# Part-filled PV rounds released and zero filler matmuls issued where a planner sees TensorE thinly used

## The chip, the cores and the metric

One core of a Trainium2 chip. The time is device microseconds (us) of one execution, lower is better; a time told here is the median of several executions of the same program. Only executions in the undisturbed ("fast") state occurred. Engines are named as the profile names them: PE is TensorE, ACT ScalarE, DVE VectorE, POOL GpSimd, SP SyncE.

## The reference

A layer normalisation of x (2048 x 512) feeds two branches: multi-query attention with 32 heads of 16 channels that share one key and one value head, and an MLP (512 to 1792 to 512). The result is `x + attention * silu(MLP)`.

```python
xn = layernorm(x)
q = (xn @ wq) in 32 heads of 16; k = xn @ wk; v = xn @ wv      # one k, one v
s = softmax(q k^T / 4) v, heads joined, @ wo
g = silu( silu(xn @ w1) @ w2 )
return x + s * g
```

The bulk is 32 x 2048 x 2048 exponentials of scores. ACT computes about three quarters of the score blocks (1556 of 2048 blocks of 128 x 512) and DVE the other 492, by a chain of integer operations.

## The kernel before

The Python code does not emit instructions directly. A planner inside it simulates the engines with fixed planned durations, decides at each step what each engine does next, and emits the resulting five fixed instruction streams with the semaphore waits that they need. A change of one rule can therefore move instructions on every engine.

PE does three kinds of work in the steady state: scores (`do_S`, up to four row tiles at once), jobs (projections and MLP, in rounds of four column tiles) and PV rounds (`do_pv`: up to four probability blocks times the values, four column tiles at once, all into one bank of PSUM, the memory that PE writes its results to, `ps` in the profile's lines). A PV round with fewer than four blocks is held back for up to 1 us:

```python
def pv_round(t):
    ... # for each of the four column tiles: the first block that is ready, into got
    if len(got) < 4 and nleft[g] > 0 and t - old < HOLD and a_pressure() < NPA - 2:
        return ("wait", min(soon, old + HOLD))
    return ("go", got)
```

At each step PE takes scores if they are due, else a job, else a PV round, else the tail; if there is nothing it waits until the next thing is ready:

```python
def pe_step():
    ...
    if pr and pr[0] == "go" and (a_pressure() >= NPA - 2):
        col = ("pv", pr[1])
    elif jr[0] == "go":
        col = ("job", jr[1])
    elif pr and pr[0] == "go":
        col = ("pv", pr[1])
    elif tr and tr[0] == "go":
        col = ("tail", None)
    ...
    if st["assigned"] < 3 and "zer" in pl.lastw and ...:      # start only: warm-up
        n = st["warm"] = st.get("warm", 0) + 1
        pl.place(PE, T_COLD if n <= N_COLD else MM, lambda pe: pe.matmul(
            bank(7), lhsT=zer_sb[:, 0:P], rhs=zer_sb[:, :], start=True, stop=True), ["zer"], [("ps", 7)], ...)
```

The planner knows a slow ("cold") matmul only there: the first `N_COLD` warm-up matmuls are planned at `T_COLD` (427 ns), everything later at `MM` (216 ns). In the profile before, the warm-up's weight loads stand 0.43 us apart until 6.73 us, and the five from 7.12 us on take 0.96 us together. Two PSUM banks, 5 and 7, form a pool for jobs and for DVE's score blocks.

## Time and profile before

| | before |
|---|---|
| median of 4 runs of the comparison | 778.38 us (776.87 to 780.08) |
| span of the profiled execution | 777.3 us |
| ACT idle in it | 28.7 us |
| of that, from 40 us to the last exponential | 8.0 us |
| mean granted PE clock of it | 0.985 |

How to read it: ACT, the busiest engine, has 748.6 us of work to do, so as long as that work stays the same only its idle time can be won. The granted clock is 1.0 at full PE clock and 0.5 at half: from 40 to 760 us of this profile it reads 0.50 for 3.4 us each from 280.1, 563.4 and 747.8 us on (a "window" in what follows), for 6.8 us, two windows, from 420.1 us on, and 1.00 elsewhere.

### The profile page before, as it was taken

What the parts mean: (1) busy time and instruction counts of PE and PEld (TensorE: products, weight loads), DVE (VectorE), ACT (ScalarE), POOL (GpSimd) and SP (SyncE); (2) the same over time, 40 slices, a digit from 0 to 9 for tenths busy, and PEclk for the clock granted to TensorE, in tenths of its full rate; (3) what the DMA queues carried; (4) which work ended last, traced back from release to release, by engine and by line L of the source; (5) the groups of instructions that cost most, each with busy time, mean ns of one, the idle gap of its engine ahead of it and who ended that gap; (6) DMA issues with size and microseconds to landing.
All of it is one profiled execution on the core that took longest, in us unless ns stands there. A gap on an engine that the chain in (4) does not pass through costs nothing.

```text
span 777.3 us, 19793 instructions
## 1 busy us (share of the span) xinstructions
PE 706.3 (91%) x8600; PEld 202.2 (26%) x8600; DVE 737.9 (95%) x1290; ACT 748.6 (96%) x760; POOL 19.9 (3%) x46
## 2 busy tenths in 40 slices
PE   8899899899989899899988998999998899999985
PEld 3322222222222222222222222222222222222221
DVE  8699999999999989999998999999999999999995
ACT  5899999999999999999998999999999999999995
POOL 5400000000000000000000000000000000000000
PEclk9999999999999999999998999999999999999999
DMA  9300000000000100000000010000000000000000
GB/s 312 84 1 2 2 1 2 2 2 2 1 2 16 29 14 2 2 2 2 2 1 1 16 42 2 2 1 2 3 2 1 15 16 29 2 1 2 2 1 28
DMA packets 11428, 12.55 MB, mean 16 GB/s; under 512 B 1808, under 2 KB 10768, under 8 KB 11344
## 3 DMA queue, kind: packets, MB, share of 16 engines
q1 hardware_dynamic: 10288, 11.28, 4.5%
q8 instruction: 68, 1.11, 0.6%
q10 hardware_dynamic: 1056, 0.03, 0.1%
q14 instruction: 16, 0.13, 0.1%
HBM read 8.95 MB, written 2.10 MB: 14 GB/s over the span
## 4 chain that ended last, share of the span: by engine, by line
ACT 80%; DVE 10%; PE 9%; issue 1%; POOL 0%; ACTq 0%; DVEq 0%
ACT pa_sb L1170 76%; DVE db_sb L869 4%; DVE ds_sb L903 3%; ACT t_sb L521 3%; PE ps L963 3%; PE ps L693 3%; PE ps L394 2%; PE ps L1146 1%; ACT t_sb L544 1%; DVE stats_sb L355 0%; DVE u_sb L523 0%; DVE f_sb L980 0%; PE ps L410 0%; POOL v_sb L478 0%; DVE qt_sb L501 0%
## 5 line engine op out<-in xcount | busy, mean ns | idle before, releaser
L1170 ACT ACTIVATE pa_sb<-ps 128x1024 bf16<-128x1024 f32 (+1 forms) x681 | 732.2, 1358 | 8.2 <-PE ps L693 4.4
L869 DVE TENSOR_SCALAR db_sb<-ps 128x512 uint16<-128x512 f32 x492 | 326.2, 681 | 17.3 <-PE ps L693 15.6
L903 DVE TENSOR_SCALAR ds_sb<-db_sb 128x2048 uint16<-128x2048 uint16 x492 | 321.6, 679 | 1.1
L693 PE MATMUL ps<-qt_sb,kt_sb 32*128 32x512 bf16 x2048 | 269.6, 387 | 53.4 <-ACT pa_sb L1170 42.7
L963 PE MATMUL ps<-ds_sb,v_sb 128*32 128x512 bf16 x1968 | 264.0, 387 | 4.0 <-DVE ds_sb L903 3.3
L963 PE MATMUL ps<-pa_sb,v_sb 128*32 128x512 bf16 x1556 | 255.3, 390 | 3.3 <-DVE ds_sb L903 2.1
L693 PEld LDWEIGHTS ps<-qt_sb,kt_sb 32*128 32x128 bf16 x2048 | 68.5, 91 | 337.8 <-ACT pa_sb L1170 275.4
L963 PE MATMUL ps<-db_sb,v_sb 128*32 128x512 bf16 x492 | 131.7, 393 | 2.9 <-DVE f_sb L980 2.4
L963 PEld LDWEIGHTS ps<-ds_sb,v_sb 128*32 128x32 bf16 x1968 | 66.3, 95 | 67.3 <-issue 35.6
L963 PEld LDWEIGHTS ps<-pa_sb,v_sb 128*32 128x32 bf16 x1556 | 62.4, 95 | 56.1 <-issue 35.4
L394 PE MATMUL ps<-xnT_sb,w_sb 128*32 128x512 bf16 x896 | 76.0, 390 | 0.1
L394 PE MATMUL ps<-w_sb,u_sb 128*32 128x512 bf16 x896 | 74.9, 384 | 0.0
L521 ACT ACTIVATE t_sb<-ps 128x512 bf16<-128x512 f32 x56 | 44.9, 802 | 1.9 <-PE ps L394 1.9
L523 DVE SCALAR_TENSOR_TENSOR u_sb<-t_sb,ps 128x512 bf16<-128x512 bf16 x56 | 38.0, 678 | 0.2 <-ACT t_sb L521 0.2
L963 PEld LDWEIGHTS ps<-db_sb,v_sb 128*32 128x32 bf16 x492 | 32.3, 95 | 20.5 <-issue 9.5
L980 DVE STREAM_TRANSPOSE f_sb<-ps 128x512 f32<-128x512 f32 x32 | 22.6, 707 | 7.7 <-PE ps L963 7.7
L394 PEld LDWEIGHTS ps<-xnT_sb,w_sb 128*32 128x32 bf16 x896 | 19.5, 94 | 29.0 <-issue 20.2
L394 PEld LDWEIGHTS ps<-w_sb,u_sb 128*32 128x32 bf16 x896 | 18.6, 94 | 29.2 <-issue 23.5
L394 PE MATMUL ps<-xnT_sb,wq_sb 128*32 128x512 bf16 x256 | 20.4, 384 | 0.2 <-DVE u_sb L523 0.2
L394 PE MATMUL ps<-wo_sb,on_sb 128*32 128x512 bf16 x256 | 19.1, 382 | 0.0
L984 DVE TENSOR_TENSOR otr_sb<-f_sb,rcp_sb 128x256 bf16<-128x256 f32 x32 | 13.2, 413 | 0.0
L544 ACT ACTIVATE t_sb<-ps 128x512 bf16<-128x512 f32 x16 | 13.0, 810 | 0.0
(42 smaller groups left out, 156.1 us busy)
## 6 DMA issues: line engine op xcount, KB each, us to landing
w_sb<-in_B_w_dram SPq DMA_DIRECT2D x2, 1792.0 KB, 13.5
xr_sb<-in_A_x_dram SPq DMA_DIRECT2D x16, 128.0 KB, 2.3
out_dram<-ob_sb SPq DMA_DIRECT2D x16, 128.0 KB, 1.7
ds_sb<-in_A_x_dram SPq DMA_DIRECT2D x3, 512.0 KB, 6.7
ds_sb<-in_A_x_dram SPq DMA_DIRECT2D x4, 128.0 KB, 2.6
wq_sb<-in_A_wq_dram SPq DMA_DIRECT2D x1, 512.0 KB, 4.8
wo_sb<-in_A_wo_dram SPq DMA_DIRECT2D x1, 512.0 KB, 15.3
kt_sb<-kt_sb SPq DMA_DIRECT2D x4, 64.0 KB, 2.4
```

The costliest lines, as they stand in the source:

```text
L394: last = h.matmul(bank(b)[32 * j:32 * (j + 1), :], lhsT=lhs(j), rhs=rhs, start=start, stop=stop, tile_position=(0, 32 * j), skip_group_che ...
L521: t1 = Task(AC, 477.0, lambda a: a.activation(t_sb[:, k, :], bank(b), ACT.Tanh, scale=0.5), [("ps", b)], [("t", k)], 0)
L523: t2 = Task(DV, T_P, lambda v: v.scalar_tensor_tensor(out=u_sb[:, ft, :], in0=t_sb[:, k, :], scalar=1.0, in1=bank(b), op0=ALU.add, op1=ALU ...
L544: t1 = Task(AC, 477.0, lambda a: a.activation(t_sb[:, k, :], bank(b), ACT.Tanh, scale=0.25), [("ps", b)], [("t", k)], 0)
L693: return pe.matmul(bank(b), lhsT=kt_sb[32 * i:32 * i + 32, g % 2, kt * P:(kt + 1) * P], rhs=qt_sb[32 * i:32 * i + 32, (g // 2) % NQR, :], ...
L869: bt.P[i] = pl.add(Task(DV, T_P, lambda v, b=b, i=i, bb=bt.b: v.tensor_scalar(db_sb[:, bb, i * NQ:(i + 1) * NQ], bank(b), 128.0 * LOG2E, 1 ...
L903: pl.add(Task(DV, T_SH, lambda v, s=s, j=j, bb=bt.b: v.tensor_scalar(ds_sb[:, s, :], db_sb[:, bb, :], SHIFT[j], None, op0=ALU.add), [("Db" ...
L963: h = pe.matmul(bank(OB)[32 * i:32 * (i + 1), :], lhsT=lhs, rhs=rhs, start=s0, stop=s1, tile_position=(0, 32 * i), skip_group_check=True)
L980: t1 = pl.add(Task(DV, T_TR, lambda v: v.transpose(f_sb[:, k, :], bank(OB)), [("ps", OB)], [("F", k)], 1, [norm.get(("m", g - 2))]))
L984: t3 = pl.add(Task(DV, 332.0, lambda v: v.tensor_tensor(o3[:, :, val:val + DH], f3[:, :, val:val + DH], rcp_sb[:, k, :].unsqueeze(2).to_br ...
L1146: pl.place(PE, T_COLD if n <= N_COLD else MM, lambda pe: pe.matmul(bank(7), lhsT=zer_sb[:, 0:P], rhs=zer_sb[:, :], start=True, stop=True), ...
L1170: op = pl.place(AC, 0.8333 * NQ * n + T_AF, lambda a: a.activation(pa_sb[:, s, 0:n * NQ], ps[:, b0 * 512:(b0 + n) * 512], ACT.Exp), [("ps" ...
```

## The change

The intent is to keep the PE clock up; that this rule does it is what the experiments test. Where the planned use of PE over the last 3 us is a half or less, a part-filled PV round goes at once, and if PE has nothing else, a round of four zero matmuls goes into a free bank of the pool. Besides, the planner is told of 14 cold warm-up matmuls instead of 10.

```diff
-T_TP, T_COLD, N_COLD = 56.0, 427.0, 10
+T_TP, T_COLD, N_COLD = 56.0, 427.0, 14
+LOW_USE, USE_WIN = 0.5, 3000.0
-            if len(got) < 4 and nleft[g] > 0 and t - old < HOLD and a_pressure() < NPA - 2:
+            if len(got) < 4 and nleft[g] > 0 and t - old < HOLD and a_pressure() < NPA - 2 and pe_share(t) > LOW_USE:
                 return ("wait", min(soon, old + HOLD))
+        def pe_share(t):          # planned use of PE over the last USE_WIN ns
+            ...
+            return s / USE_WIN
+        def fill_bank(t):         # None above LOW_USE, else a free pool bank
+            ...
+        def do_fill(t, b):
+            pl.place(PE, MM, lambda pe: col4(pe, b, lambda j: zer_sb[:, 32 * j:32 * (j + 1)], zer_sb[:, :], True, True),
+                     ["zer"], [("ps", b)], t0=pe_start(t, "C"))
+            ...
             elif tr and tr[0] == "go":
                 col = ("tail", None)
+            elif st["assigned"] > 0 and not tail["made"]:
+                fb = fill_bank(t)
+                if fb is not None:
+                    col = ("fill", fb)
```

More of the change, by code (lines that the diff above doesn't have):

```diff
@@ L1098, in a_pressure @@
             return sum(1 for b in pa_busy if b)
+        def pe_share(t):
+            s = 0.0
+            for op in reversed(pl.order[PE]):
+                if op.end <= t - USE_WIN:
+                    break
+                s += op.end - max(op.t0, t - USE_WIN)
+            return s / USE_WIN
+        def fill_bank(t):
+            if "zer" not in pl.lastw or pe_share(t) > LOW_USE:
+                return None
+            for b in pool_free:
+                if pl.ready(PE, ["zer"], [("ps", b)]) <= t:
+                    return b
+            return None
+        def do_fill(t, b):
+            pl.place(PE, MM, lambda pe: col4(pe, b, lambda j: zer_sb[:, 32 * j:32 * (j + 1)], zer_sb[:, :], True, True),
+                     ["zer"], [("ps", b)], t0=pe_start(t, "C"))
+            pl.mode = "C"
+            st["fills"] = st.get("fills", 0) + 1
         def pe_step():
@@ L1134, in pe_step @@
                     do_job(t, col[1])
+                elif col[0] == "fill":
+                    do_fill(t, col[1])
                 else:
```

## The prediction

> **What bounds the kernel now.** I began with the first part of the page, the busy shares, and then the chain of waits that ended last.
>
> ```profile
> span 777.3 us, 19793 instructions
> ...
> PE 706.3 (91%) x8600; PEld 202.2 (26%) x8600; DVE 737.9 (95%) x1290; ACT 748.6 (96%) x760; POOL 19.9 (3%) x46
> ...
> ACT 80%; DVE 10%; PE 9%; issue 1%; POOL 0%; ACTq 0%; DVEq 0%
> ```
>
> ScalarE (ACT) is the bound: it is idle for 777.3 - 748.6 = 28.7 us in all, and the chain lies on it for 80% of the span. TensorE (PE) looks 91% full, but the table of waits has it waiting for ACT's exponentials for longer than for all else together:
>
> ```profile
> PE ps L693 <- ACT pa_sb L1170: 42.7, 113, 1.0
> ```
>
> So PE has slack, and its work costs time only where it makes ACT wait. I therefore split ACT's 28.7 us by stretches of 20 us. Up to 20 us ACT is busy for 10.70 of 20 (9.3 us idle: loads, normalisation, transposes, first keys), from 20 to 40 us for 18.05 (1.95 idle), and after its last exponential, at about 767.9 us, it is idle for 9.4 us (last normalisation, output product, write). That leaves 28.7 - 9.3 - 1.95 - 9.4 = 8.0 us for the 728 us in between. This is all that a steadier PE could win in the steady state. The stretches of 20 us (PE, weight loads, DVE, ACT, POOL, then PEclk):
>
> ```profile
> 240.00:260.00 20.00, 18.03 (x239) 5.16 (x235) 20.00 (x36) 18.82 (x22) 0.00 (x0) 1.00 0.05 15
> ...
> 280.00:300.00 20.00, 19.66 (x231) 5.16 (x227) 17.54 (x30) 19.34 (x22) 0.00 (x0) 0.91 0.01 2
> ...
> 380.00:400.00 20.00, 17.45 (x221) 5.14 (x222) 19.95 (x34) 18.25 (x20) 0.00 (x0) 1.00 0.00 1
> ...
> 420.00:440.00 20.00, 19.73 (x215) 5.07 (x219) 17.56 (x32) 17.68 (x19) 0.00 (x0) 0.83 0.05 15
> ...
> 560.00:580.00 20.00, 17.77 (x209) 4.86 (x208) 18.96 (x34) 19.32 (x20) 0.00 (x0) 0.91 0.00 1
> ...
> 740.00:760.00 20.00, 16.50 (x168) 4.12 (x166) 18.88 (x34) 19.07 (x18) 0.00 (x0) 0.91 0.00 1
> ```
>
> Two of these six lose ACT time at the full clock (240 and 380 us: 1.18 and 1.75 us, with DVE at 20.00 and 19.95 of 20, so DVE led there). In the other four PE's granted clock fell. The worst, in steps of 2 us:
>
> ```profile
> 416.00:418.00 2.00, 1.05 (x11) 0.31 (x11) 2.00 (x5) 2.00 (x4) 0.00 (x0) 1.00 0.00 0
> 418.00:420.00 2.00, 1.37 (x18) 0.38 (x16) 0.99 (x2) 2.00 (x3) 0.00 (x0) 1.00 0.00 0
> 420.00:422.00 2.00, 2.00 (x16) 0.38 (x16) 1.97 (x4) 1.71 (x2) 0.00 (x0) 0.52 0.00 0
> 422.00:424.00 2.00, 2.00 (x18) 0.55 (x18) 1.80 (x6) 2.00 (x3) 0.00 (x0) 0.50 0.00 0
> 424.00:426.00 2.00, 2.00 (x24) 0.40 (x16) 0.77 (x2) 0.86 (x1) 0.00 (x0) 0.50 0.00 0
> 426.00:428.00 2.00, 2.00 (x26) 0.63 (x22) 1.78 (x3) 1.13 (x1) 0.00 (x0) 0.77 0.00 0
> ```
>
> Read it downwards: PE is lightly used for 4 us while it waits for ACT (11 and 18 matmuls instead of about 24), then runs at half clock for about 6.8 us, and at the end of that ACT starves. The timeline puts 0.29 + 2.01 = 2.30 us of ACT idle into this stretch, 0.16 + 0.51 = 0.67 into the one at 280 us, 0.17 + 0.51 = 0.68 into that at 564 us, and the stretch at 747 us shows 0.93. Sum: 4.6 us of ACT idle that goes with a halved clock. That is the target of the change.
>
> [...]one window of 3.4 us at half clock in 20 us gives 1 - 0.5 x 3.4/20 = 0.915 (the rows say 0.91), two give 0.83 (as at 420 us).[...] In the trace the weight loads of the warm-up stand at 2.03, 2.46, 2.89, 3.31 us and so on up to 6.73, 0.43 apart, and the five from 7.12 us on take 0.96 us together.[...]
>
> **The change part by part.** The order of instructions of both built kernels gives the counts.
>
> Work: scores (2048 matmuls), PV (492 + 1968 + 1556), jobs and every DVE instruction are equal in number. ACT reads 485 x 2 + 195 x 3 + 1 = 1556 score blocks before and 481 x 2 + 198 x 3 = 1556 after, in 679 instead of 681 instructions: nothing that counts. The first PE difference after the start is near the 177th score, so the whole plan is reshuffled from there on.
>
> Warm-up: telling the planner of 14 cold matmuls instead of 10 makes it place 16 of them before the first transposes instead of 20. This is on the path (the chain begins with these 20, 7.37 us):
>
> ```profile
> 1.21 7.37 PE L1146 MATMUL ps<-zer_sb 128*128 128x512 bf16 x20 [1.21 <-DVE zer_sb L335]
> ...
> 7.37 1.54 DVE L371 TENSOR_SCALAR xn_sb<-ds_sb,mv_sb,rstd_sb 128x512 bf16<-128x512 bf16 x4 [0.49 <-POOL rstd_sb L367]
> ...
> 8.41 0.61 PE L410 MATMUL ps<-ident,xn_sb 128*128 128x128 bf16 x8
> ```
>
> Four warm ones less are 4 x 0.21 = 0.85 us. But the first normalised tile is ready only at 7.37 + 1.54/4 = 7.76 us, so the transposes can begin at about 8.0 to 8.1 instead of 8.41. After that the three ACT copies of 0.58 us set the pace. Gain 0.35 us, all on the path.
>
> Fillers: 11 rounds of four, 44 matmuls. The timeline has 16 job matmuls in 1.05 us, so a round costs (1.05 - 0.39)/3 = 0.22 us: 11 x 0.22 = 2.4 us of PE, into its 777.3 - 706.3 = 71 us of idle. They go where the plan is thin, so I charge 0.1 us a round of possible lateness to none but those that meet a score: under 0.3 us in all. In the trace of before, the score at which they stand falls at 140 (twice), 518, 562 (twice), 696, 733, 746, 747, 749 and 764 us. Five of the eleven are within 2 us of the starts of the dips at 564 and 747 us; none is near 280 or 420 us.
>
> Rounds not held: the scheduler's list has 1054 PV rounds before, 120 of them part-filled, and 1062 after, 131 part-filled. 8 x 0.22 = 1.8 us more PE, again in slack. This part acts on the dips at 280 and 420 us. The quantity that the change tests, the planned use of PE over the last 3 us (a share, from the plan's lists), has its deepest valleys before at 0.29 to 0.33, five in number; four of them are the stretches with the four dips. After, the same four places have valleys of 0.43 to 0.44, and only one valley, near the end, is as deep as 0.32.
>
> Sum: of the 4.6 us I take 80% as won (3.7), as one dip may stay or a new one may appear[...]; 0.35 from the start; less 0.3 for fillers in the way. 3.7 + 0.35 - 0.3 = 3.75 us. 777.7 - 3.7 = 774.0 us.
>
> **The rivals.** First: nothing happens, because a dip's loss is only delayed work and ACT then waits for DVE, busy 95%. For it: at 240 and 380 us ACT lost time at full clock with DVE at 20 us of 20, and DVE's total is equal in both kernels. Against it: during the dips DVE is idle too (1.3 of 2 us at 280). This would give 777. Second: the fillers and small rounds delay scores and ACT waits for PE at the full clock. For it: ACT's units are short and each of the 679 needs a score round in time. Against it: outside the dips PE waits for ACT. If each of 19 extra rounds cost its 0.22 us, 4.2 us would be lost and the gain gone: 778. Third: [...]the planned valleys at half use still trip the clock, and one or two dips of 0.7 to 2.3 us come at other places: 775 to 777. Fourth: all dips go and the reshuffled order also closes the DVE-led waits: 777.7 - 8.0 - 0.35 = 769.3 us, the floor.
>
> **Range and chances.** Centre 774.0. The first three rivals make 777 the upper end; all dips gone with some luck in the order makes 771 the lower. Faster by 2% needs 762.1 us, below the floor of 769.3: 0.01. Slower by 2% needs 15.6 us more, four times what all extra rounds cost: 0.01. Within 2%: 0.98.
>
> **What would show it.** Right: no stretch of 20 us from 40 to 760 us with a clock under 0.95, or one at most; ACT idle there near 4 us instead of 8.0; first transposes near 8.05 us and first exponential near 12.8 instead of 13.15; ACT's busy time within 1 us of 748.6. Wrong: dips as many as before with the time unchanged (third rival); no dips and the same ACT idle, now put down to DVE (first) or to scores at full clock (second); or a longer end, where the last transposition on DVE waited 6.6 us for PV rounds.

## The result, and the profile after

| | before | after |
|---|---|---|
| median of the runs | 778.38 us (4 runs) | 774.21 us (4 runs, 772.44 to 775.11) |
| ratio | | 0.9943, 95% interval 0.9915 to 0.9972 |
| span of the profiled execution | 777.3 us | 773.3 us |
| ACT idle | 28.7 us | 25.9 us |
| ACT idle, 40 us to the last exponential | 8.0 us | 4.3 us |
| mean granted clock of the profiled execution | 0.985 | 0.993 |

A ratio here is the mean time of one kernel's fast runs over that of the other's fast runs of the same rounds, so it is not quite the ratio of the medians. The gain is 0.6%: clear of noise, and the same within 2%. The profiled execution was the slowest of the four; the other three had a clock of 0.997.

The page of the changed kernel (its lines for the span and busy time, and for the chain of waits):

```profile
span 773.3 us, 19855 instructions
...
PE 704.9 (91%) x8640; PEld 202.7 (26%) x8640; DVE 738.3 (95%) x1290; ACT 747.4 (97%) x758; POOL 19.9 (3%) x46
...
ACT 88%; DVE 6%; PE 5%; DMA 1%; issue 0%; SPq 0%; ACTq 0%; DVEq 0%
```

PE's busy share has not moved at all; a reader of that line alone would think that nothing had happened. The chain now lies on ACT for 88% instead of 80%. The stretches of 20 us tell where (columns as before: length, PE, weight loads, DVE, ACT, POOL, granted clock, share of the DMA engines, GB/s):

```profile
240.00:260.00 20.00, 18.83 (x240) 5.26 (x237) 19.83 (x35) 20.00 (x22) 0.00 (x0) 1.00 0.05 15
...
280.00:300.00 20.00, 18.71 (x235) 5.41 (x235) 18.45 (x33) 20.00 (x22) 0.00 (x0) 1.00 0.01 2
...
380.00:400.00 20.00, 18.43 (x235) 5.36 (x235) 19.82 (x35) 20.00 (x21) 0.00 (x0) 1.00 0.01 2
...
420.00:440.00 20.00, 18.95 (x241) 5.30 (x238) 19.79 (x35) 20.00 (x22) 0.00 (x0) 1.00 0.06 15
...
500.00:520.00 20.00, 18.52 (x215) 4.70 (x211) 18.07 (x31) 19.07 (x20) 0.00 (x0) 0.91 0.00 1
520.00:540.00 20.00, 18.90 (x244) 5.21 (x236) 20.00 (x36) 18.65 (x20) 0.00 (x0) 1.00 0.01 2
...
560.00:580.00 20.00, 19.00 (x251) 5.50 (x243) 19.84 (x35) 20.00 (x22) 0.00 (x0) 1.00 0.01 2
...
720.00:740.00 20.00, 17.47 (x213) 5.14 (x209) 19.32 (x34) 18.70 (x20) 0.00 (x0) 1.00 0.01 2
740.00:760.00 20.00, 16.88 (x188) 4.68 (x185) 16.90 (x30) 19.87 (x19) 0.00 (x0) 1.00 0.00 1
```

All four stretches that had lost clock (280, 420, 560, 740 us) are at 1.00, with ACT at 19.87 to 20.00 instead of 17.68 to 19.34. One new half-clock window stands at 513 us. The two losses at full clock (240, 380 us) are gone, but others have come (1.35 us at 520, 0.48 at 580 and 1.30 us at 720 us): that is the reshuffled order, and it nets to nothing. From 40 to 760 us ACT's idle time in stretches at full clock sums to 3.40 us in both profiles; in stretches that lost clock it fell from 4.59 to 0.93.

Account of the profiled pair, ACT idle before and after: up to 20 us 9.3 and 10.98, from 20 to 40 us 1.95 and 1.07, from 40 us to the last exponential 7.99 and 4.33, after it 9.44 and 9.46. So the middle gave 3.66 us, the start lost 0.8, and ACT's busy time fell by 1.2; together the 4.0 us of the span. The fall of ACT's busy time, with two instructions fewer, was not pursued.

### The profile page after: what moved, and what is told of

Read it like the earlier page. It is cut to its first block, busy times and chain, and to the rows that moved or that the text cites. A ratio compares the mean times of both kernels' runs of the same rounds, so it can differ in the third digit from the quotient of the medians.

```text
span 773.3 us, 19855 instructions
## 1 busy us (share of the span) xinstructions
PE 704.9 (91%) x8640; PEld 202.7 (26%) x8640; DVE 738.3 (95%) x1290; ACT 747.4 (97%) x758; POOL 19.9 (3%) x46
## 4 chain that ended last, share of the span: by engine, by line
ACT 88%; DVE 6%; PE 5%; DMA 1%; issue 0%; SPq 0%; ACTq 0%; DVEq 0%
ACT pa_sb L1200 83%; ACT t_sb L523 3%; DVE db_sb L871 2%; DVE ds_sb L905 2%; PE ps L965 1%; PE ps L695 1%; PE ps L396 1%; ACT t_sb L546 1%; DMA ds_sb<-in_A_x_dram 1%; DVE stats_sb L357 1%; PE ps L438 0%; SPq L315 0%; PE ps L412 0%; DVE f_sb L982 0%; DVE qt_sb L503 0%
## 5 line engine op out<-in xcount | busy, mean ns | idle before, releaser
L965 PE MATMUL ps<-ds_sb,v_sb 128*32 128x512 bf16 x1968 | 258.5, 384 | 2.3 <-DVE ds_sb L905 1.7
L965 PE MATMUL ps<-pa_sb,v_sb 128*32 128x512 bf16 x1556 | 245.7, 386 | 2.3 <-DVE ds_sb L905 1.5
L396 PE MATMUL ps<-xnT_sb,w_sb 128*32 128x512 bf16 x896 | 72.5, 384 | 0.7 <-DVE db_sb L871 0.4
L523 ACT ACTIVATE t_sb<-ps 128x512 bf16<-128x512 f32 x56 | 47.5, 848 | 0.0
L546 ACT ACTIVATE t_sb<-ps 128x512 bf16<-128x512 f32 x16 | 13.0, 815 | 0.0
```

Source lines behind the costliest of these rows:

```text
L396: last = h.matmul(bank(b)[32 * j:32 * (j + 1), :], lhsT=lhs(j), rhs=rhs, start=start, stop=stop, tile_position=(0, 32 * j), skip_group_che ...
L523: t1 = Task(AC, 477.0, lambda a: a.activation(t_sb[:, k, :], bank(b), ACT.Tanh, scale=0.5), [("ps", b)], [("t", k)], 0)
L546: t1 = Task(AC, 477.0, lambda a: a.activation(t_sb[:, k, :], bank(b), ACT.Tanh, scale=0.25), [("ps", b)], [("t", k)], 0)
L965: h = pe.matmul(bank(OB)[32 * i:32 * (i + 1), :], lhsT=lhs, rhs=rhs, start=s0, stop=s1, tile_position=(0, 32 * i), skip_group_check=True)
```

## The experiments

The first theory (clock) is that the gain is the ACT idle behind windows of half PE clock, and that the fillers remove the windows; where the work stands is a side matter. The rivals are that the new order of PV rounds closes waits at full clock (order), that the mere presence of instructions helps (presence), and that the shorter warm-up helps (start). Runs of one group shared their runs of the kernel before.

| run | order of the real work | fillers | runs | median us | ratio to before (95%) | median clock |
|---|---|---|---|---|---|---|
| before, first group | before | none | 43 | 779.29 | 1 | 0.984 |
| e1 the changed kernel again | after | 11 rounds | 6 | 773.18 | 0.9910 (0.9885 to 0.9934) | 0.997 |
| e2 slipped in | before | 14 rounds | 6 | 773.64 | 0.9924 (0.9900 to 0.9948) | 0.9955 |
| e3 fillers dropped | after | none | 22 | 777.37 | 0.9973 (0.9960 to 0.9987) | 0.988 |
| e4 warm-up count alone | before | none | 22 | 779.52 | 0.9995 (0.9981 to 1.0008) | 0.986 |
| e5 tiny fillers | before | 14 rounds of 16 columns | 14 | 778.80 | 1.0000 (0.9984 to 1.0016) | 0.986 |
| e6 all gaps filled | before | 140 rounds | 6 | 772.71 | 0.9922 (0.9906 to 0.9937) | 0.997 |
| e7 filler rule alone | a third one | 22 rounds | 6 | 774.04 | 0.9944 (0.9926 to 0.9962) | 0.998 |
| e8 released, slipped in below 0.65 | after, without planned fillers | 53 rounds | 6 | 772.13 | 0.9913 (0.9897 to 0.9928) | 0.998 |
| e9 q copy first, on the change | a fourth one | by the rule | 14 | 778.37 | 0.9992 (0.9976 to 1.0009) | 0.991 |
| e10 q copy first, on e8 | a fifth one | slipped in | 15 | 781.28 | 1.0028 (1.0012 to 1.0043) | 0.991 |

e1 to e4, e5 to e8, and e9 and e10 are the three groups, each on another chip. The kernel before had a median of 779.29 us in the first, 778.36 (19 runs, clock 0.986) in the second and 778.47 (28 runs, 0.986) in the third; a ratio is to the runs of its own group. All results were correct.

**e1: the changed kernel again.** No edit.

> The changed kernel once more, as the measure for the others of this chip. Ratio to the kernel before 0.994 to 0.996, near 774 us, mean clock of its runs about 0.997 against 0.985 to 0.988 before.

It came out 6.1 us ahead of the kernel before, more than the first comparison's 4.2; the interval, 0.9885 to 0.9934, lies wholly below the 0.994 to 0.996 that was expected. Of these 1.9 us more, 0.9 lie in the median of the kernel before (779.29 against 778.38) and 1.0 in that of the changed kernel (773.18 against 774.21). The wider spread is the kernel before's. Its 43 runs of this group, sorted by their mean clock:

| mean clock of the run | runs | median us |
|---|---|---|
| 0.978 | 4 | 782.91 |
| 0.982 | 4 | 782.00 |
| 0.984 | 14 | 779.42 |
| 0.986 | 7 | 779.14 |
| 0.991 | 10 | 777.25 |

(Four runs in between left out.) The same program, and its time follows its clock: a straight line through the 43 runs has a correlation of -0.93 and 4.4 us for each 0.01 of clock. From 0.984 to the changed kernel's 0.997 that is 0.013 x 437 = 5.7 us of the 6.1. One window of 3.4 us at half clock, as in the profile before, is worth 0.5 x 3.4/778 = 0.0022 of mean clock, so about 1.0 us by this line; the ACT idle of the five windows in the first profile, 4.6 us, gives 0.9 each. How many windows a run of the kernel before catches differs from run to run: in the second group one run of it had a clock of 0.997, and it took 774.77 us, near the changed kernel's time. This is a correlation; the next runs are the tests.

**e2: fillers slipped into the unchanged order.** In the kernel before, a filler round is placed without planned duration in a planned PE gap of at least 216 ns where the planned use, fillers counted, is a half or less. The planned times of all other instructions are the same to the nanosecond, and PE's order apart from zero matmuls is identical.

```diff
+        def slip(t, b):
+            last = pl.order[PE][-1]
+            op = pl.place(PE, 0.0, lambda pe: col4(pe, b, ... zer_sb ...), ["zer"], [("ps", b)], t0=t)
+            op.t0 = op.end = last.end          # the plan does not see it
+            slipped.append((t, t + MM))
 ...
+            if st["assigned"] > 8 and not tail["made"] and INF > nxt >= t + MM and (not slipped or slipped[-1][1] <= t):
+                fb = fill_bank(t)
+                if fb is not None:
+                    slip(t, fb)
             return nxt
```

> The order of the kernel before on every engine, unchanged, with 14 filler rounds (56 zero matmuls) slipped into PE gaps of at least 216 ns of its plan where the planned use is under a half. Clock theory (the 4 us are the ACT idle behind half-clock windows, whatever the order): the windows of low clock at 280, 420, 564 and 747 us go or become fewer, mean clock 0.992 or more, ratio 0.995 to 0.997 (774.5 to 776 us). Order theory (the reshuffled order closes waits at full clock, the clock is a bystander): same order, so ratio 1.000, 778 us.

Ratio 0.9924: most of the gain with none of the new order. Three of the four low stretches of before are at full clock, and ACT is full in them; the last kept one window:

```profile
280.00:300.00 20.00, 19.35 (x239) 5.31 (x239) 18.66 (x32) 20.00 (x23) 0.00 (x0) 1.00 0.00 1
...
420.00:440.00 20.00, 19.69 (x261) 5.61 (x262) 19.95 (x36) 20.00 (x22) 0.00 (x0) 1.00 0.05 15
...
560.00:580.00 20.00, 18.59 (x237) 5.09 (x235) 19.98 (x35) 20.00 (x22) 0.00 (x0) 1.00 0.01 2
...
740.00:760.00 20.00, 17.09 (x178) 4.39 (x182) 15.32 (x27) 19.25 (x18) 0.00 (x0) 0.91 0.00 1
```

The losses at full clock of the order before are still there (at 240 and 380 us ACT has 18.81 and 18.24 of 20 in this profile), as they must be if only the clock was treated. The order theory, which said 1.000, falls as the main cause.

**e3: the order after, its fillers dropped.** The plan is that of the changed kernel; the 11 filler rounds are removed from PE's list before emission, and the waits that they held pass to the next PE instruction.

```diff
+        drop = {id(o) for o in fillers}
+        ...                                    # deps of a dropped one go to the next PE instruction
+        pl.order[PE] = kept
```

> The order of the changed kernel on every engine, with its 11 filler rounds left out of the emitted program (their planned places stay empty), so the released PV rounds and the warm-up count act alone. If the fillers carry the gain: one or two half-clock windows return (near 511, 555 or 740 us), mean clock 0.990 or so, 776 to 777 us, ratio 0.998. If the released rounds and the new order carry it: clock and time as the changed kernel, 774 us, ratio 0.995.

Ratio 0.9973 at a clock of 0.988. Windows come back. In the profiled run, which at 779.75 us and a clock of 0.984 was one of the slowest of the 22, they stand at 500 us (one) and 740 us (two), and most of two between 20 and 40 us:

```profile
20.00:40.00 20.00, 18.46 (x218) 7.46 (x210) 11.96 (x30) 17.44 (x17) 8.68 (x21) 0.85 0.26 71
...
500.00:520.00 20.00, 18.20 (x214) 4.58 (x206) 18.12 (x32) 19.08 (x21) 0.00 (x0) 0.91 0.01 2
...
740.00:760.00 20.00, 17.07 (x167) 4.15 (x167) 17.84 (x31) 18.19 (x17) 0.00 (x0) 0.83 0.01 2
```

At 280 and 420 us there is no loss in this profile, nor in the two of the changed kernel, which have no filler near these places. In the three profiles of the order before without full-width fillers (before, e4, e5) a window stands at 420 us each time and at 280 us twice. So the new order, with its released rounds, probably took those two valleys away; three profiles a side can't exclude luck. The order is worth about 0.3% (with the warm-up count in it) and the fillers, 0.991 against 0.9973, about 0.6%. The order's part seems to come by the clock as well: ACT's idle time at full clock from 40 to 760 us is 3.30 us here, against 3.40 in the kernel before. How much of it is the released rounds and how much the rest of the reshuffle, no run separates.

**e4: the warm-up count alone.** The order is that of before but for four warm-up matmuls.

```diff
-T_TP, T_COLD, N_COLD = 56.0, 427.0, 10
+T_TP, T_COLD, N_COLD = 56.0, 427.0, 14
```

> The kernel before with the warm-up count alone (20 cold matmuls in all instead of 24, the order otherwise the same). Start theory: first exponential 0.35 us earlier than in the profile before, ratio 0.9995. Rival: the start hangs on when the x loads arrive[...], so no difference that can be told from noise, ratio 1.000, first exponential between 12.8 and 13.7 us.

Ratio 0.9995 with an interval that holds 1: nothing that can be told. The first exponential stood at 13.54 us in its profile, later than the 13.15 of before. This profile shows something else as well. The stretch from 140 us, in the kernel before (first fence) and here (second):

```profile
140.00:160.00 20.00, 18.80 (x239) 5.10 (x236) 19.82 (x35) 19.87 (x21) 0.00 (x0) 1.00 0.01 2
```

```profile
140.00:160.00 20.00, 19.29 (x219) 4.95 (x223) 17.65 (x31) 17.71 (x19) 0.00 (x0) 0.83 0.00 1
```

Both have the same order of work and the same thin PE there (the fifth of the valleys in the prediction). In one execution it cost nothing, in the other two windows of half clock and 2.2 us more of ACT idle. So the same order lost clock there in one execution (0.83) and not in the other (1.00).

**e5: the same fillers, 16 columns instead of 512.** Same places, same number of instructions, same waits and weight loads as e2.

```diff
-            op = pl.place(PE, 0.0, lambda pe: col4(pe, b, ... rhs zer_sb[:, :] ...),
+            def emit(pe):                      # four column tiles, as col4
+                h = pe.matmul(bank(b)[32 * j:32 * (j + 1), 0:16], lhsT=..., rhs=zer_sb[:, 0:16], ...)
```

> As e2 (order of before, 14 filler rounds at the same places, the same waits and the same 56 instructions) but each zero matmul streams 16 columns instead of 512[...]. Clock theory[...]: no gain, the low windows stay, mean clock about 0.986, ratio 0.999 to 1.001 (779 us). Rival (the presence of instructions, or the waits that the fillers take early, is what helps): the gain of e2 stays, ratio 0.992 to 0.995.

Ratio 1.0000, clock 0.986 as in the kernel before. Its profile keeps windows at 280, 420 and 740 us (the first two straddle the edge of a stretch, so part of each is in the row before):

```profile
420.00:440.00 20.00, 19.70 (x249) 5.41 (x249) 19.11 (x34) 19.16 (x21) 0.00 (x0) 0.95 0.05 15
...
740.00:760.00 20.00, 16.93 (x178) 4.41 (x175) 16.78 (x29) 19.25 (x18) 0.00 (x0) 0.91 0.00 1
```

The presence of the instructions gains nothing that can be told. A filler matmul has a median of 178 ns in this profile, against 384 ns with 512 columns in e2's. With rounds of 512 columns the clock was 1.00 in three of the four places (e2); with rounds of 16 it was at 1.00 in one of them (560 us); what lies between was not tried.

**e6: every gap filled.** As e2, with the limit on use taken away: 560 zero matmuls.

```diff
-LOW_USE, USE_WIN = 0.5, 3000.0
+LOW_USE, USE_WIN = 1.5, 3000.0
```

> Dose: order of before, with zero matmuls in every planned PE gap of 216 ns or more that has a free bank (140 rounds, 31 us of PE). Clock theory: no low window from 40 to 760 us, mean clock 0.997 or more, so at least e2's ratio (0.992) if fillers never stand in the way of a score round; rival (fillers in the way): each late filler pushes a score round by up to 0.2 us, ACT waits at full clock, and the ratio goes back to 0.996 or above although the clock is full.

Ratio 0.9922 and clock 0.997. Ten times the fillers cost nothing measurable (PE busy 727.8 us of its 770.9 in the profile) and win little more than e2's 14 rounds. In the profile all stretches from 40 to 760 us have a clock of 1.00, so no window is left there to win.

**e7: the filler rule alone.** The change without the released rounds and without the new warm-up count. Here the fillers take planned time, so they reshuffle the plan; it gave DVE 16 instructions more (1306).

```diff
 # against the changed kernel
-T_TP, T_COLD, N_COLD = 56.0, 427.0, 14
+T_TP, T_COLD, N_COLD = 56.0, 427.0, 10
-... and a_pressure() < NPA - 2 and pe_share(t) > LOW_USE:
+... and a_pressure() < NPA - 2:
```

> The kernel before with the change's filler rule alone (22 rounds in a plan that they reshuffle; rounds held as before, 10 cold warm-up matmuls). Clock theory: low windows rare, mean clock 0.994 or more, ratio 0.992 to 0.995. If an unlucky reshuffle costs ACT waits at full clock, 0.996 to 1.0 at the same clock.

Ratio 0.9944 at a clock of 0.998, as good as any here. With the clock full as in e6, the time is 1.3 us longer. In the profile ACT waits at full clock in eleven stretches from 40 to 760 us, 7.90 us in all against e6's 3.54; DVE's 16 more instructions go with 3.1 us less work on ACT (744.5 us busy against 747.7), which hides most of it. So a reshuffled plan can bring several microseconds of waits apart from the clock; that the orders before and after cost the same 3.40 us is a property of this pair.

**e8: a try for a better one.** Released rounds and warm-up count of the change, no planned fillers, and fillers slipped in wherever the planned use is below 0.65.

```diff
 # against the changed kernel; slip as in e2
+SLIP_USE = 0.65
-            elif st["assigned"] > 0 and not tail["made"]:      # planned fillers
+            elif False:
+            if st["assigned"] > 8 and not tail["made"] and INF > nxt >= t + MM and ...:
+                slip(t, fb)
```

> A try for a better one: the order of the change without its planned fillers (PV rounds released under a half, warm-up 14), and fillers slipped without displacing anything into gaps wherever the planned use is under 0.65 (53 rounds). Clock theory with the order's own share of 0.997 (e3): 0.990 to 0.991, near or just under the changed kernel, 772 us, clock 0.997. If fillers get in the way: 0.993 or above.

Ratio 0.9913, as the changed kernel's 0.9910. It is a cleaner way to the same end (fillers can't displace anything in the plan), not a faster one that these runs could prove.

**e9 and e10: the start.** With the shorter warm-up worth nothing in e4, I looked at what sets the first score. In the changed kernel's profile PE's first transposes stand at 7.21 us, 1.2 us earlier than before, yet the first score comes later. DVE's row tells why:

```profile
9.86 1.29 DVE L357 BATCH_NORM_STATS2 stats_sb<-ds_sb 128x6 f32<-128x512 bf16 x2 [1.25 <-DMA ds_sb<-in_A_x_dram]
...
11.14 0.66 DVE L357 BATCH_NORM_STATS2 stats_sb<-ds_sb 128x6 f32<-128x512 bf16 x1
...
11.80 0.66 DVE L357 BATCH_NORM_STATS2 stats_sb<-ds_sb 128x6 f32<-128x512 bf16 x1
...
12.44 0.69 DVE L503 TENSOR_SCALAR qt_sb<-ps 128x512 bf16<-128x512 f32 x1
...
13.18 0.39 PE L695 MATMUL ps<-qt_sb,kt_sb 32*128 32x512 bf16 x3 [1.67 <-DVE qt_sb L503]
```

DVE waits 1.25 us for the load of the second block of x, does four statistics on it, and only then copies q out of PSUM, for which the scores wait 1.67 us. So I held those statistics until the q copy stands in DVE's order, in the changed kernel (e9) and in e8 (e10):

```diff
-  gate=(lambda: q_done.get(0) is not None and q_done[0].op is not None) if j > 1 else
-  (lambda: ("xnT", 3) in pl.lastw) if j > 0 else None))
+  gate=(lambda: q_done.get(0) is not None and q_done[0].op is not None) if j > 0 else None))
```

> The changed kernel with the statistics of the second x block held until the first q copy stands in DVE's order, so that copy no longer waits behind four statistics (2.6 us) and their load. If that row is what set the first score in the changed kernel: first exponential near 12.0 to 12.4 us instead of 12.8 to 13.6, and up to 1 us off the time if the later second block starves nothing: ratio 0.990. Rival (the second block's keys come later and ACT waits for them at 20 to 40 us instead): first exponential early, ACT idle from 20 to 40 us up by about as much, ratio 0.991 to 0.993.

> The same on the kernel of e8 (released rounds, fillers slipped in under 0.65). If it adds up: 0.990, 771 us, clock 0.998. If the start gives back what it won, or the reshuffle costs ACT waits: 0.991 to 0.994.

Neither gains: 0.9992 and 1.0028, both above what either of their forecasts allowed. The first exponential came at 12.73 and 12.23 us, earlier as intended, but then ACT stood still for 3.1 us until scores with the second block's keys came (e9, ACT's row: start, length, and the idle time before with what ended it):

```profile
12.73 4.62 ACT L1199 ACTIVATE pa_sb<-ps 128x1536 bf16<-128x1536 f32 x4
17.65 1.45 ACT L1199 ACTIVATE pa_sb<-ps 128x1536 bf16<-128x1536 f32 x1 [0.29 <-PE ps L694]
22.20 3.28 ACT L1199 ACTIVATE pa_sb<-ps 128x1024 bf16<-128x1024 f32 x3 [3.10 <-PE ps L694]
```

The rival that was written down for them names the right wait: the start gives back what it won, and more. But that is the smaller part. In the profiles e9's span is 7.3 us longer than e1's: 2.8 us of it is ACT idle up to 40 us, 3.2 us ACT idle from 40 to 760 us, and 1.4 us more ACT work. Two of e9's stretches lost clock (0.84 from 40 us, with 1.99 us of ACT idle, and 0.91 from 160 us, with 1.72), although the filler rule was on; its first filler stands at 145.1 us. e10's span is 8.5 us longer than e8's, with 2.0 us more ACT idle up to 40 us and 6.9 us more from 40 to 760 us; 8.73 us of its idle time there lie in stretches at full clock, against e8's 3.43. So there it was mostly the order that cost time, and less the clock. Why these orders wait more was not taken apart.

## Why the prediction was right, point by point

The predicted 774.0 us met 774.21. That it met it this closely is partly luck: the prediction took 3.75 us off the 777.7 us of the runs known then, the first comparison shows 4.2 us off 778.38, and e1 6.1 us off 779.29. The mechanism is confirmed by tests that separate it: the order of before with fillers gains (e2), the order of after without them loses most of the gain (e3), fillers of 16 columns gain nothing (e5). Some terms of the sum were mis-sized, and they partly cancelled.

- **The dips, "of the 4.6 us I take 80% as won (3.7)".** In the profiled pair ACT idle from 40 us on fell by 3.66 us, all of it in stretches that had lost clock (4.59 to 0.93). But 80% of what one profile showed was a low figure for the kernel before as a whole. Its profiled run had a clock of 0.985, the runs of the first group 0.978 to 0.991, and a valley that was free in the profile, at 140 us, cost 2.2 us in e4. By the line through the 43 runs the clock is worth 5.7 us against the changed kernel. I had taken windows at other places as a risk to the gain only; they are as much a loss that the kernel before has in runs I had not seen.
- **The start, "gain 0.35 us, all on the path".** This step failed. e4 measured 0.9995 with an interval from 0.9981 to 1.0008, and the profiles don't bear it out: with 16 warm-up matmuls the first exponential stands at 12.77 us in e1, near the predicted 12.8, but at 13.49 to 13.62 in the other four (after, e3, e4, e8), against 12.93 to 13.15 with 20. Two things took its place: the 20 warm-up matmuls, 7.37 us long in the profile before, took 5.96 to 6.69 us in three other profiles with 20 (e2, e5, e6), so it was that execution's longer slow spell that put them on the path (weight loads 0.43 us apart until 6.73 us, in e2 until 4.17 us); and the q copy stands behind four statistics on DVE, which in three of the five profiles with 16 wait for a load (1.25 us in after, 0.85 in e3, 0.93 in e4).
- **The fillers in the way, "less 0.3".** Nothing that can be told: e6 put 140 rounds into the order of before and stayed at 0.9922.
- **"None is near 280 or 420 us", the released rounds act there.** It fits: in e3, without fillers, these two stretches are clean. But e2 shows that fillers alone clear them too. The sizes are 0.3% for the order with its released rounds and 0.6% for the fillers.
- **The rivals.** The first (ACT then waits for DVE) is wrong: where the clock came back, ACT was at 19.87 to 20.00 of 20. The second (rounds in the way) is refuted by e6. The third was real: one window at 513 us in the profile, and about 1 us for it. The fourth did not come: the two DVE-led waits were closed, and two of 1.3 us and one of 0.5 opened elsewhere.
- **What would show it.** One stretch below 0.95 and ACT idle of 4.3 against "near 4" came as told. First transposes at 8.05 us and first exponential at 12.8 did not (7.21 and 13.62), and ACT's busy time fell by 1.2 us where 1 was told as the limit.

## What to carry to other kernels

When the engine that bounds a kernel shows short idle spots, put the granted PE clock beside them by stretches: here a thin spell of PE (29 matmuls from 416 to 420 us) was followed by 6.8 us at a clock of 0.50, and ACT, another engine, was idle for 2.30 us in it. Zero matmuls of full width in gaps that the schedule has anyway were a cheap cure here (e2, ratio 0.9924), if not a complete one (one window stayed at 747 us in e2's profile, one came at 513 us in the changed kernel's). Slip them in so that they move nothing else: orders that the change of a rule had reshuffled cost up to 5 us more of waits at full clock (e7, e10). Compare the clocks of many runs first: here the runs of one unchanged kernel differ by as much as the whole change brings, and a single profile shows only one of these executions.

## What the traces show of the PE clock

- Before the falls PE was thin, not idle. In the profile before, the 3.4 us ahead of the four falls at 280.1, 420.1, 563.4 and 747.8 us have 21 to 24 matmuls each, five or six rounds of four, and a PE busy time of 1.93 to 2.08 us; at the 0.22 us a round worked out in the prediction that is an estimate of 32 to 39% of that stretch. In the changed kernel's profile the fall at 513.0 us has 25 matmuls and 2.23 us ahead of it. A thin stretch alone does not tell: from 139.5 to 142.9 us the profile before has 22 matmuls and 1.92 us, and its clock stayed at 1.00 there. What sets these apart, and where a limit lies, was not measured.
- The recorded clock does not show the slow warm-up. The profile before gives 1.00 for the first 20 us although the warm-up's weight loads stand 0.43 us apart until 6.73 us. In the profile after they stand so until 4.17 us, under a recorded 1.00 as well; the 0.87 for its first 20 us comes from a later spell (0.68 from 14 us, 0.50 from 16 to 20 us). So a mean clock leaves out a part that differed by 2.6 us between these two profiles, an estimate of 0.5 x 2.6/777 = 0.002. At the fall at 420.1 us the record agrees with the timeline: the six rounds of four that stand on a line of their own from 420.3 to 425.8 us take 0.61 to 0.64 us each, against 0.39 to 0.40 us for three at a clock of 1.00 (560.4 to 562.1 us).
- What the fillers were mattered. Rounds of four 32-column tiles on zeros went with a median clock of 0.9955 and a ratio of 0.9924 when 512 columns wide (e2), and with 0.986 and 1.0000 when 16 columns wide (e5).
